# Issuing the r and v loads of the first three steps from the ScalarE DMA queue in a fused RWKV-6 and squared-ReLU kernel

## The chip, the cores and the metric

The kernel runs on one core of one Trainium2 chip. The metric is the device time in microseconds of that core. A profile of one execution gives the span from the first to the last instruction, which is a little shorter than the device time.

## The reference

Two layers are computed one after the other. The first is a linear attention with a decaying state (B, H, S, D = 4, 8, 768, 48):

```python
for t in range(S):
    cur = einsum('bhd,bhe->bhde', u[None] * kt, vt)
    y[:, :, t] = einsum('bhd,bhde->bhe', rt, state + cur)
    state = wt[:, :, :, None] * state + einsum('bhd,bhe->bhde', kt, vt)
```

Its output is laid out as 3072 tokens by 384 and goes through `maximum(x @ w_in, 0)`, a square, and `@ w_out`, with w_in 384 x 2048 and w_out 2048 x 384. All inputs and outputs are float32.

## The kernel before, in words

The attention is worked off in 24 steps, each one chunk of 128 tokens of one batch entry with all eight heads: six steps follow one another through the state, then the next batch entry begins. A step needs four loads of 192 KB, w, r, k and v, in rows of 48 floats (192 bytes). Its work is cut into small functions, one per engine and stage:

- ScalarE: `lw_` (L149, logarithm of w), `exp_` (L184 and L185), `v_` (L153, v to bf16), `xt_` (L273, the finished chunk into `xT`).
- PE: `cum_` (L176 to L179, cumulative sums of the logarithm), `tr_` (L198), `p_` (L210), `su_` (L225), `y_` (L247, L255), `yt_` (L270).
- DVE: `rd_` (L189), `rkt_` (L202), `pm_` (L216), `ts_` (L232, L234), `q_` (L165), `ysb_` (L261).
- GpSimd (POOL): `ku_` (L157), `qp_` (L161), `vq_` (L169), `sn_` (L238).

The second layer works on blocks of one or two finished chunks: `m1_` (L288, PE) gives groups of 512 columns of hidden values, `rl_` (L295, ScalarE) takes the ReLU, `gt_` (L300, DVE) the square, `m2_` (L307, PE) the second product in four quarters, `os_` (L312, ScalarE) the copy out of PSUM, and `store` (L316) writes 192 KB. A first-layer matmul over a block of two chunks has 256 columns ("wide"), over one chunk 128 ("narrow"). `m1_` has two PSUM buffers, so its third group needs the ReLU of the first.

The weights come in eight loads of 768 KB, four of w_in (`load_wi`, L95) and four of w_out (`load_wo`, L101), and are cast to bf16 by `cast` (L108); the first and third of each go to ScalarE, the second and fourth to DVE.

All loads and stores are issued on SyncE (SP), in one row. The loads stand in the order of `seq`: w, r, k, v of step 0, u, the four of step 1, four of w_in, the four of step 2, four of w_out, then step after step. `A_IN = 7` buffers hold each raw input.

The order of all engines' work is made while the program is built. `op` enters each piece with its engine, an assumed duration, a rank and what it depends on; `make_order` then plays the engines forward in time, gives each free engine its lowest-ranked ready piece, and writes down the resulting order, which each engine later follows instruction by instruction. A load on SP is assumed to take 1.25 us (2.08 for weights) and to be there when it ends. Where PE would stand idle before the first `m2_`, `warm_` matmuls (L321), whose result is not used, are put in.

Of the kernel before, what the change touches and what calls it, by code (L numbers as in the profile page):

```python
# [9 lines left out]
FP32 = mybir.dt.float32  # L10
# [7 lines left out]
def kernel(  # L18
# [11 lines left out]
    nc = tc.nc  # L30
    PSUM = bass.MemoryType.PSUM

    B, H, S, D = r.shape
    C = 128
# [10 lines left out]
    A_IN = 7  # L45
    HOP = .2
    PACE = 0.0

    nc.scalar.preload_act_table_set("natural_log_exp_and_others")

# [3 lines left out]
    a_in = ctx.enter_context(tc.tile_pool(name="a_in", bufs=A_IN))  # L54
# [10 lines left out]
    ps_m2 = ctx.enter_context(tc.tile_pool(name="ps_m2", bufs=1, space=PSUM))  # L65


    def load_one(dst, src, b, c):
        nc.sync.dma_start(  # L69
            out=dst, in_=src[b, :, c * C:(c + 1) * C, :].rearrange("h c d -> c h d"))  # L70

    raw = {}

    def load_step(step, part):
        b, c = divmod(step, NCH)
        if part == "w":
            raw["w", step] = a_in.tile([C, H, D], FP32, name="w_raw")
            load_one(raw["w", step][:], w, b, c)
        elif part == "r":
            raw["rk", step] = a_in.tile([C, 2, H, D], FP32, name="rk_raw")  # L80
            load_one(raw["rk", step][:, 0], r, b, c)
        elif part == "k":
            load_one(raw["rk", step][:, 1], k, b, c)
        else:
            raw["v", step] = a_in.tile([C, H, D], FP32, name="v_raw")
            load_one(raw["v", step][:], v, b, c)

    wi_sb = weights.tile([C, KT, DFF], BF16)
    wo_sb = weights.tile([C, NT, DM], BF16)
# [238 lines left out]
    def op(eng, us, rank, fn, args, deps, take=None, give=None):  # L328
        key = (fn.__name__,) + args
        plan[key] = (eng, us, rank, fn, args, deps, take, give)  # L330

    def steps(s, *names):
        return [(n, s) for n in names] if s >= 0 else []

    for s in range(NSTEP):
        c, at = s % NCH, s * 100
# [25 lines left out]
    for kind, cols in (("i", KT), ("o", 4)):  # L362
        for g in range(4):
            for j in range(cols):
                eng = "AV"[g % 2]
# [29 lines left out]
    def ld(n, x):  # L395
        {"i": load_wi, "o": load_wo}.get(x, lambda g: load_u() if x == "u" else load_step(g, x))(n)

    last = []
    for n, x in seq:
        free = steps(n - A_IN, *{"w": ("lw_",), "r": ("rd_", "qp_"), "v": ("v_", "vq_")}.get(x, ()))  # L400
        op("S", {"i": 2.08, "o": 2.08, "u": .65}.get(x, 1.25), 0, ld, (n, x), last + free)
        last = [("ld", n, x)]

    def make_order():
        hop, pace, pace_from = HOP, PACE, 5
        free_at = dict(P=0.0, V=0.0, A=1.5, G=0.0, S=2.35)
        psum = {x: [0.0] * n for x, n in dict(cp=1, tr=1, y=1, m1=2, m2=1, rl=3).items()}
        waits = {k: [d for d in plan[k][5] if d in plan] for k in plan}
        todo = {e: sorted((k for k in plan if plan[k][0] == e), key=lambda k: plan[k][2])
                for e in free_at}  # L410
        done, order, times, next_cum = {}, [], [0.0, 1.5, 2.35], 0.0
        while any(todo.values()):
            now = heapq.heappop(times)
            for e in free_at:
                if free_at[e] > now + 1e-6:
                    continue
                for key in todo[e]:
                    _, us, _, fn, _, _, take, give = plan[key]
                    deps = waits[key]
                    if any(d not in done or  # L420
                           done[d] + (hop if plan[d][0] != e else 0) > now + 1e-6 for d in deps):
                        continue
                    if take and not (psum[take] and min(psum[take]) < now + 1e-6):
                        continue
                    if fn is cum_ and key[1] >= pace_from:
                        if now < next_cum - 1e-6:
                            heapq.heappush(times, next_cum)
                            continue
                    if fn is cum_:
                        next_cum = now + pace  # L430
                    if take:
                        psum[take].remove(min(psum[take]))
                    end = done[key] = free_at[e] = now + us
                    if give:
                        psum[give].append(end + hop)
                        heapq.heappush(times, end + hop)
                    heapq.heappush(times, end)
                    heapq.heappush(times, end + hop)
                    order.append((now, key))
                    todo[e].remove(key)  # L440
                    break
        first_m2 = min(t for t, k in order if k[0] == "m2_")
        at = 0.0
        for t, key in [x for x in order if plan[x[1]][0] == "P"]:
            if at < first_m2:
                n = int((t - at - .1) / (.215 if at > 7 else .43))
                if n > 0 and t <= first_m2:
                    order.append((at + 1e-4, ("warm_", n)))
            at = done[key]
        return sorted(order, key=lambda x: x[0]), done  # L450

    order, done = make_order()
    E = mybir.EngineType
    with tc.manual_schedule(engines={E.PE, E.DVE, E.Activation, E.Pool, E.SP}):
# [34 lines left out]
```

## Time and profile before

| | us |
|---|---|
| device time, median of 2 runs | 219.09 (218.32 to 219.87) |
| span of the profiled execution | 214.2 |
| PE busy, share of the span | 197.1 (92%) |
| PE busy with `warm_` matmuls (L321) | 17.9 |
| DVE busy | 152.7 (71%) |
| ACT busy | 127.5 (60%) |
| POOL busy | 84.1 (39%) |
| chain that ended last: PE, SP's queue, DMA, DVE | 46%, 13%, 13%, 10% |
| first `m1_` matmul begins | 21.65 |
| last step load is issued | 142.11 |

The profiled execution's own device time is not listed apart from the two runs; the median stands 4.9 us above the span. "Busy" counts the time in which an engine works on an instruction. An instruction that issues a DMA is not counted as busy; it is shown under SPq for SyncE. L numbers are lines of the kernel before. A share of the DMA engines is the mean over 16 of them, and can pass 1 in a short stretch, since the packets of a transfer overlap.

### The profile page before, as it was taken

The page shows a single profiled execution, that of the slowest core. Times are in us where ns is not written, and L with a number is a line of the kernel's source. Part 1 is how long each engine was busy: PE and PEld are TensorE (multiplying, and loading weights), DVE is VectorE, ACT ScalarE, POOL GpSimd, SP SyncE. Part 2 cuts the span into 40 slices and gives each one's busy share as a digit, 9 for nine tenths or more (in the row PEclk, how much of TensorE's full clock was granted, in tenths as well). Part 3 has the DMA queues.
Part 4 walks back from the last instruction along what each step waited for, and adds up shares of the span by engine and source line. Part 5 has one row for each costly group of instructions (what it writes and reads, how often), then busy time and mean ns, then how long its engine had stood idle before and what let it go on. Part 6 is the DMA issues. An engine that isn't in the chain of part 4 may idle for free.

```text
span 214.2 us, 5655 instructions
## 1 busy us (share of the span) xinstructions
PE 197.1 (92%) x2232; PEld 140.4 (66%) x2232; DVE 152.7 (71%) x279; ACT 127.5 (60%) x255; POOL 84.1 (39%) x105
## 2 busy tenths in 40 slices
PE   7898997987899997989999999999999999999983
PEld 2454765555677675766766677777777777777751
DVE  3475795646898989879859989989886775533310
ACT  3353966644856767477685576667847546555540
POOL 5371320546556639655565655557112010000000
PEclk9999999999999999999999999999999999999999
DMA  7999899779987999699889997983101100111112
GB/s 135 195 307 344 207 383 219 153 164 193 177 152 150 181 163 171 135 200 160 172 167 195 142 203 147 193 176 76 40 2 41 37 11 28 40 37 37 40 37 73
DMA packets 107177, 30.43 MB, mean 142 GB/s; under 512 B 100368, under 2 KB 105616, under 8 KB 107152
## 3 DMA queue, kind: packets, MB, share of 16 engines
q1 hardware_dynamic: 107152, 30.09, 67.1%
q8 instruction: 17, 0.28, 0.6%
q14 instruction: 8, 0.07, 0.1%
HBM read 25.36 MB, written 4.72 MB: 140 GB/s over the span
## 4 chain that ended last, share of the span: by engine, by line
PE 46%; SPq 13%; DMA 13%; DVE 10%; issue 7%; POOL 6%; ACT 3%; DVEq 0%; POOLq 0%
PE m L307 19%; PE m L288 17%; SPq L69 10%; DMA w_st<-in_moe_w_out_dram 4%; DVE gt L300 4%; DMA w_raw<-in_w_dram 3%; DMA v_raw<-in_v_dram 3%; POOL qprod L161 2%; DVE pmT L216 2%; PE tr L198 2%; POOL ku L157 2%; DMA rk_raw<-in_r_dram 2%; POOL vq L169 2%; PE cp L210 1%; SPq L95 1%
## 5 line engine op out<-in xcount | busy, mean ns | idle before, releaser
L288 PE MATMUL m<-xT,wi_sb 128*128 128x256 bf16 (+1 forms) x672 | 76.5, 257 | 4.2 <-ACT xT L273 2.9
L295 ACT ACTIVATE rl<-m 128x512 f16<-128x512 f32 x96 | 56.5, 597 | 37.5 <-PE m L288 36.4
L307 PE MATMUL m<-wo_sb,gt 128*128 128x384 bf16 x384 | 74.9, 326 | 1.2 <-ACT o_sb L312 0.6
L288 PEld LDWEIGHTS <-wi_sb 128*128 128x128 bf16 x672 | 57.7, 98 | 17.1 <-issue 5.4
L300 DVE TENSOR_TENSOR gt<-rl 128x512 bf16<-128x512 f16 x96 | 54.7, 584 | 19.8 <-ACT rl L295 19.2
L307 PEld LDWEIGHTS <-gt 128*128 128x128 bf16 x384 | 35.3, 98 | 19.7 <-DVE gt L300 1.3
L157 POOL TENSOR_TENSOR ku<-rk_raw,u_bc 128x384 f32<-128x384 f32 x24 | 24.8, 1034 | 42.1 <-DMA rk_raw<-in_k_dram 37.3
L216 DVE TENSOR_TENSOR pmT<-cp,tri_strict 128x512 bf16<-128x512 f32 x48 | 30.8, 681 | 3.6 <-PE cp L210 3.6
L189 DVE TENSOR_TENSOR rdec_buf<-rk_raw,cp 128x768 bf16<-128x768 f32 x24 | 22.8, 948 | 11.2 <-ACT cp L185 9.0
L169 POOL TENSOR_TENSOR vq<-v_raw,q 128x384 f32<-128x384 f32 x24 | 21.6, 901 | 18.8 <-DVE y_sb L261 8.6
L161 POOL TENSOR_TENSOR qprod<-rk_raw,ku 128x384 f32<-128x384 f32 x24 | 25.1, 1048 | 1.2
L238 POOL TENSOR_TENSOR S<-t_state,a_c 128x192 bf16<-128x192 f32 x20 | 11.0, 548 | 29.3 <-DVE t_state L234 16.7
L185 ACT ACTIVATE cp<-cp 128x768 f32<-128x768 f32 x24 | 19.1, 795 | 0.8
L321 PE MATMUL m<-warm 128*128 128x512 bf16 x64 | 17.9, 416 | 1.2 <-DVE warm L129 1.2
L202 DVE COPY rkT<-tr 128x1024 bf16<-128x1024 bf16 x24 | 16.4, 682 | 3.7 <-PE tr L198 3.7
L149 ACT ACTIVATE lw_buf<-w_raw 128x384 bf16<-128x384 f32 x24 | 12.5, 521 | 8.4 <-DMA w_raw<-in_w_dram 8.2
L153 ACT CAST v_bf<-v_raw 128x384 bf16<-128x384 f32 x24 | 12.2, 508 | 8.4 <-DMA v_raw<-in_v_dram 7.7
L312 ACT ACTIVATE o_sb<-m 128x384 f32<-128x384 f32 x24 | 11.8, 491 | 8.2 <-PE m L307 7.6
L165 DVE TENSOR_REDUCE q<-qprod 128x8 f32<-128x384 f32 x24 | 13.1, 545 | 4.4 <-POOL qprod L161 4.1
L198 PE MATMUL tr<-ident,rdec_buf 128*128 128x128 bf16 x192 | 14.8, 220 | 1.3 <-DVE rdec_buf L189 1.0
L261 DVE TENSOR_TENSOR y_sb<-vq,y 128x384 bf16<-128x384 f32 x24 | 13.1, 547 | 2.2 <-PE y L255 2.1
L198 PEld LDWEIGHTS <-rdec_buf 128*128 128x128 bf16 x192 | 11.5, 98 | 4.1 <-DVE rdec_buf L189 2.0
(40 smaller groups left out, 142.9 us busy)
## 6 DMA issues: line engine op xcount, KB each, us to landing
w_raw<-in_w_dram SPq DMA_DIRECT2D x24, 192.0 KB, 4.3
rk_raw<-in_r_dram SPq DMA_DIRECT2D x24, 192.0 KB, 4.2
rk_raw<-in_k_dram SPq DMA_DIRECT2D x24, 192.0 KB, 4.3
v_raw<-in_v_dram SPq DMA_DIRECT2D x24, 192.0 KB, 4.1
out_dram<-o_sb SPq DMA_DIRECT2D x24, 192.0 KB, 2.0
w_st<-in_moe_w_in_dram SPq DMA_DIRECT2D x4, 768.0 KB, 8.5
w_st<-in_moe_w_out_dram SPq DMA_DIRECT2D x4, 768.0 KB, 8.6
u_bc<-in_u_dram SPq DMA_DIRECT2D x1, 192.0 KB, 4.6
```

The lines of the kernel that those rows point to most:

```text
L69: nc.sync.dma_start(out=dst, in_=src[b, :, c * C:(c + 1) * C, :].rearrange("h c d -> c h d"))
L157: nc.gpsimd.tensor_mul(ku[:], raw["rk", s][:, 1], u_bc[:])
L161: nc.gpsimd.tensor_mul(qp[:], raw["rk", s][:, 0], tiles.pop(("ku", s))[:])
L169: nc.gpsimd.tensor_mul(vq[:], raw["v", s][:], tiles.pop(("q", s))[:, :, None].to_broadcast([C, H, D]))
L185: nc.scalar.activation(cs[:, :, 0:DM], cs[:, :, 0:DM], AF.Exp)
L189: nc.vector.tensor_mul(rdec[:, :, :, 0:D], raw["rk", s][:], tiles.pop(("cs", s))[:, :, 0:DM].rearrange("p a (h d) -> p a h d", h=H))
L198: nc.tensor.transpose(ps_tr[:, i, p, :], rdec[:, i, 2 * p:2 * p + 2, :], ident[:])
L216: nc.vector.tensor_mul(tiles["pmT", s][:, e], tiles["p", s][:, e].rearrange("p (a t) -> p a t", a=HP), tri_strict[:, None, :].to_broadcast ...
L288: nc.tensor.matmul(ps1[:, j, :], wi_sb[:, kk, n * 128:(n + 1) * 128], xT[:, kk, s0 * C:s0 * C + width], start=(kk == 0), stop=(kk == KT - 1))
L295: nc.scalar.activation(rl[:], tiles.pop(("m1", i, g))[:], AF.Relu, scale=RS)
L300: nc.vector.tensor_mul(tiles["gt", i][:, g * ng:(g + 1) * ng, :], rl[:], rl[:])
L307: nc.tensor.matmul(tiles["m2"][:], gt[:, n, mt * 128:(mt + 1) * 128], wo_sb[:, n, :], start=(n == 0), stop=(n == NT - 1))
```

## The change

A constant `TWO = 3` names the first three steps. Their r and v loads are issued from ScalarE's DMA queue, and are planned there; w and k, and all later loads, stay on SP. In the plan such a load takes 0.5 us of ScalarE and is there 2.5 us later; v is entered as depending on r of its step.

```diff
+    TWO = 3
...
-    def load_one(dst, src, b, c):
-        nc.sync.dma_start(
+    def load_one(dst, src, b, c, eng=None):
+        (eng or nc.sync).dma_start(
...
         elif part == "r":
-            raw["rk", step] = a_in.tile([C, 2, H, D], FP32, name="rk_raw")
-            load_one(raw["rk", step][:, 0], r, b, c)
+            if ("rk", step) not in raw:
+                raw["rk", step] = a_in.tile([C, 2, H, D], FP32, name="rk_raw")
+            load_one(raw["rk", step][:, 0], r, b, c, nc.scalar if step < TWO else None)
         elif part == "k":
+            if ("rk", step) not in raw:
+                raw["rk", step] = a_in.tile([C, 2, H, D], FP32, name="rk_raw")
             load_one(raw["rk", step][:, 1], k, b, c)
         else:
             raw["v", step] = a_in.tile([C, H, D], FP32, name="v_raw")
-            load_one(raw["v", step][:], v, b, c)
+            load_one(raw["v", step][:], v, b, c, nc.scalar if step < TWO else None)
...
+        if x in "rv" and n < TWO:
+            op("A", .5, -100, ld, (n, x), [("ld", n, "r")] if x == "v" else [])
+            continue
         op("S", {"i": 2.08, "o": 2.08, "u": .65}.get(x, 1.25), 0, ld, (n, x), last + free)
...
-                    end = done[key] = free_at[e] = now + us
+                    end = free_at[e] = now + us
+                    if fn is ld and e == "A":
+                        end += 2.5
+                    done[key] = end
```

## The prediction

> **What bounds the kernel now.** I read the page first, then the waits and the chain, then the order of time of SP's queue and of ScalarE in the first 50 us, then the windows. The slices of the page (5.36 us each) give the outline:
>
> ```profile
> PE   7898997987899997989999999999999999999983
> ...
> DVE  3475795646898989879859989989886775533310
> ...
> DMA  7999899779987999699889997983101100111112
> ```
>
> There are three stages. Up to about 40 us the DMA engines are full and PE's digits contain stand-in work: L321's `warm` matmuls fill 17.9 us. From 60 to 117 us DVE is at 8 to 9. From 117 us PE is full and the chain holds only matmuls. So the end is set by how much useful matmul work PE has behind it when it becomes full. What is lost early is lost for good, unless PE later gets to work where it waits now.
>
> The windows of the start (columns: stretch, length, the granted clock, DMA busy share, GB/s) ask whether one issuing queue starves the DMA engines:
>
> ```profile
> 1.00:2.00 1.00, 1.00 0.07 15
> 2.00:3.00 1.00, 1.00 1.10 208
> 3.00:4.00 1.00, 1.00 1.13 215
> ...
> 15.00:16.00 1.00, 1.00 1.02 373
> ...
> 22.00:23.00 1.00, 1.00 0.48 96
> ```
>
> It does not: from 2.0 us the share is 1.0, small loads run at about 205 GB/s (192 KB in 0.96 us), weight loads at 370 to 400. Up to 35 us only the second at 22 us is half empty. The first nine loads have landed by about 11.9 us, (11.9 - 2.0) / 9 = 1.1 us each; a weight load takes about 2.4.
>
> ScalarE and SP in order of time show what the first useful block waits for:
>
> ```profile
> 12.30 5.18 SPq L69 DMA_DIRECT2D rk_raw<-in_r_dram  x1
> 17.53 4.29 SPq L69 DMA_DIRECT2D rk_raw<-in_k_dram  x1
> ...
> 20.09 1.14 ACT L108 CAST wi_sb<-w_st 128x512 bf16<-128x512 f32 x2 [3.18 <-DMA w_st<-in_moe_w_in_dram]
> ...
> 21.13 0.47 ACT L273 COPY xT<-tr 128x384 bf16<-128x384 bf16 x1
> ...
> 21.65 1.47 PE L288 MATMUL m<-xT,wi_sb 128*128 128x256 bf16 x12 [1.02 <-ACT xT L273]
> ```
>
> The second xT copy stands behind two casts that waited for the third w_in load; half a microsecond later `m1_` begins. SP's 5.18 and 4.29 us are r and k of step 2, held up while the weight loads drain. Then the chain between 38 and 49 us:
>
> ```profile
> 38.21 0.44 ACT o_sb L312
> 39.13 3.32 DMA w_raw<-in_w_dram
> 42.47 0.52 ACT lw_buf L149
> 42.99 0.39 ACT o_sb L312
> 43.80 2.99 DMA v_raw<-in_v_dram
> 46.81 0.51 ACT v_bf L153
> ```
>
> Here loads of step 4 stand behind a store on SP, and the store waits for its o_sb. That leaves holes in the DMA stream (share 0.29 in 38 to 40 us, 0.27 in 43 to 44).
>
> **What the Trainium skill says.** "DMA: Bandwidth & Descriptors", section "Issuing engines are not separate DMA queues": loads from different engines run on the same 16 DMA engines, and several issuers save only "the time on the sequencer it takes to initiate the DMA". The trace agrees as far as it goes: with one issuer the share is already 1.0 from 2 us. The same page, "Queues, rings and completion order": each DMA engine alternates between the queues packet by packet. No run here shows it yet; I use it for the landing order. The section "Anatomy of one DMA — SWDGE (gpsimd) path" says that a semaphore wait is spent on the issuing sequencer. So a load that waits blocks its engine; the chain above shows that on SP.
>
> **The change part by part.** Time does not follow from the diff alone: the planner now counts six loads off SP, so it reorders every engine. I read the built instruction order.
>
> *Issues.* Six loads leave SP and six join ScalarE. On SP they cost 0.57, 0.85, 0.61, 0.70, 5.18 and 0.61 us, but with the DMA engines full nothing starts earlier: gain at the front 0, at most the 0.5 us hole at 22 us. On ScalarE I take 0.6 to 0.85 us each, 4.3 in all. Low end: hidden, since ScalarE is busy 5.6 of the first 15 us. High end: r2's 5.18 if an issue gets stuck here too.
>
> *Waits on ScalarE.* The build gives all loads eight completion semaphores in turn, and a load waits for the previous user of its own. ScalarE's queue begins: table load, r0, r1, r2, v0 (waits for w0), `lw_`(0), v1 (waits for u), `exp_`(0), v2 (waits for w1), `lw_`(1), `v_`(0), `v_`(1), `exp_`(1). The table load ends at 2.01, three issues end at 4.3, v0 at 5.0, so `lw_`(0) starts at 5.0 for 3.83. u is third on SP beside r0 and r1 and lands near 8 (8.1 before), so `exp_`(0) goes from 5.94 to 8.8. w1 lands near 10; v1 near 14.5, since r2 and v0 share the engines with it; `exp_`(1) starts near 15 for 12.1. By itself this is hidden, because of the next item.
>
> *First `m1_`.* On PE `cum_`(2) now stands ahead of `yt_`(1) and the first `m1_`; on ScalarE all six w_in casts, then `lw_`(2), xT(0), `exp_`(2), stand ahead of xT(1). So w of step 2 now gates it, and w2 lands after all w_in. Before, w2 landed at 11.75 + 10.9 = 22.65. Now r2 and v2 move ahead of it: 2 x 1.1 = 2.2, so 24.9. Then lw 0.52, `cum_` 0.6, a_c and exp 1.0, xT 0.47, with 0.1 to 0.2 between engines: 28.0 for 21.65, **6.3 us later**.
>
> *To 46 us.* ScalarE next places four casts of the first w_out load, three relus, and four casts of the third w_out load (landing 33.35 before, and the same bytes lie ahead of it now). With two `m1` buffers PE gets five groups out and waits until about 35.9. `cum_`(3) follows at 36.8, then `m2_`. Following both orders with the trace's durations, at 46 us both are at `su_`(4). Before has done 48 wide and 48 narrow `m1` matmuls and 44 `m2`; after has 48, 36 and 16. The gap is 12 x 0.056 + 28 x 0.163 = **5.2 us of PE work**.
>
> *Recovery to `cum_`(6).* In both orders the same MLP work stands ahead of it: 90 wide-equivalent `m1` and 48 `m2`. After, left from 46.1 us: 24 x 0.11 + 32 x 0.163 = 7.9 of MLP and about 3.5 of attention, so 57.5 without a wait. Before was there at 55.86, with up to 3 us of waits on the way. The loads of steps 4 and 5 now come before the first store (22 step loads ahead of it, not 16), so I charge 1.1 us of waits: 58.6, **+2.7**. Ends: 1.6 and 5.
>
> *`cum_`(6) to `cum_`(12).* Before this took 39.6 us, with DVE work of 6 x 4.37 + 19 x 0.584 = 37.3 (the page's means: rdec 0.948, rkT 0.682, two pmT 1.362, q 0.545, y_sb 0.547, and t_state 0.35 in five steps of six). After has 18 squares: 36.7, so -0.6. But 1.9 us less MLP stands ahead of `cum_`(12) (198 and 100, not 204 and 108), and stays for the PE-bound rest: **+1.3**.
>
> *Stores further back.* Every store now has 2 to 9 more loads ahead of it, which shortens stalls like those in the chain. DVE waits 3.3 us for qprod between 60 and 120 us, and qprod waits for k's load; I credit a quarter, **-0.8**. Ends: 0 and the 6.6 us that DVE is idle there.
>
> Sum: 2.7 + 1.3 - 0.8 = +3.2. The profiled span of 214.2 becomes 217.4. The median of 219.09 has 4.9 us more than that span around it; kept, this is **222.3 us**.
>
> **Rivals.** *Nothing lasting (219.5).* The late start is absorbed: PE waits about 7 us between 46 and 120 us (8.2 from 40 us on, by the windows, some 1 of it before 46). For it: the 5.2 us deficit is mostly `m2`, needing neither ScalarE nor DVE at its start. Against it: queues are fixed, and DVE is near full in that stretch.
>
> *Faster (about 217.2).* Mechanism: stores no longer hold up loads. Place: SP, 38 to 110 us. Price: PE's 7.1 us of waits there, all gone: 5.2 - 7.1 = -1.9. It decides from the point where more than the 5.2 us comes back. For it: the chain above, and the stores' new places. Against it: much of that waiting is for DVE's own work.
>
> *Much slower (227).* An issue on ScalarE gets stuck as on SP (5.18 us) and holds `lw_`(1), `exp_`(1) and the casts, or late loads meet orders planned for early ones all through: 3 to 6 us more. For it: the weights' queue is deep at 10 us. Against it: until w2 lands near 25 there is slack of several microseconds.
>
> The change not doing what it says is excluded by the built order: the six loads are on ScalarE.
>
> **How the numbers follow.** Main case (2 to 6 us lost, 221 to 225, centre 222.3): 0.50. Much slower: 0.20. Nothing lasting: 0.18. Faster: 0.12. 2% is 4.4 us, about what a measurement of this kernel can tell from no change: limits 214.7 and 223.5. Slower: all of 0.20 and two fifths of 0.50, 0.40. Faster: a third of 0.12, 0.04. Rest 0.56. The range leaves out most of the faster case and the upper half of the much slower one: 217.0 to 228.0.
>
> **What would show it.** Right: DMA share still 1.0 from 2 us, the six issues on ScalarE, `exp_`(0) near 8.8, w2 near 25, the first `m1_` near 28 and directly after xT(1), third w_out landing unmoved near 33, PE behind by about 5 us of `m2` at 46. From 60 us DVE as full as before. Wrong: first `m1_` at 22 to 24, or PE without waits between 46 and 100 us, or loads landing more than 1 us earlier up to 35 us.

## The result, and the profile after

The changed kernel took 225.01 us (median of 2 runs, 223.59 to 226.43) against 219.09 before. The ratio is 1.0379, with a 95% interval of 1.0269 to 1.0489; it is made from undisturbed executions alone, so it is not the quotient of these medians. A later repetition gave 1.035 (1.0302 to 1.0399). The profiled span grew from 214.2 to 221.6 us, by 7.4, where 3.2 had been forecast. The profiled execution of the changed kernel took 223.59, so 2.0 us lie around its span, and not the 4.9 that the prediction had added from the median of before.

The slices of the page after (5.54 us each). L numbers of profiles after are lines of the changed kernel; from `cast` on they are four higher than in the kernel before.

```profile
PE   7560999996998888999999999997999999999983
...
DVE  3322689975878987999988998697775875333310
...
PEclk9966799999999999999999999999999999999999
DMA  8999999718979989969968969960111010100101
GB/s 133 209 356 306 330 328 171 126 38 144 190 148 166 199 144 196 176 145 176 188 139 182 201 141 189 198 130 0 38 37 38 1 38 36 38 36 36 38 36 71
```

Three things are new. PE's fourth slice (17 to 22 us) is empty, and the granted clock falls to 0.6 and 0.7 around it. DMA falls to a share of 0.1 in the ninth slice (44 to 50 us), where the kernel before has 0.85. And PE is not full for good from 117 us, but only from about 155: between 149 and 155 us it is busy 4.57 of 6 us, where the kernel before has 6.00.

The windows of the start (stretch, length, granted clock, DMA share, GB/s) answer those of before:

```profile
1.00:2.00 1.00, 1.00 0.07 14
2.00:3.00 1.00, 1.00 0.99 183
3.00:4.00 1.00, 1.00 1.29 247
15.00:16.00 1.00, 1.00 1.09 350
22.00:23.00 1.00, 0.50 1.46 200
```

A second issuing queue brings no more data per microsecond at the start; only the hole at 22 us is filled. This is what the Trainium skill's "DMA: Bandwidth & Descriptors", section "Issuing engines are not separate DMA queues", leads one to expect. What changes is which bytes come first. The order of time on ScalarE (ACTq are the issues, the brackets give the idle time before an instruction and what ended it):

```profile
7.64 0.38 ACTq L70 DMA_DIRECT2D v_raw<-in_v_dram  x1
...
9.25 0.76 ACTq L70 DMA_DIRECT2D v_raw<-in_v_dram  x1
...
19.29 0.51 ACT L157 CAST v_bf<-v_raw 128x384 bf16<-128x384 f32 x1 [7.07 <-DMA v_raw<-in_v_dram]
...
19.91 0.80 ACT L189 ACTIVATE cp<-cp 128x768 f32<-128x768 f32 x1
...
22.78 0.51 ACT L157 CAST v_bf<-v_raw 128x384 bf16<-128x384 f32 x1 [2.08 <-DMA v_raw<-in_v_dram]
...
23.20 3.21 ACT L112 CAST wi_sb<-w_st 128x512 bf16<-128x512 f32 x6
```

v of step 1 is issued at 7.64 and needs 11.6 us to land, v of step 2 13.5; before, v of step 1 took 4.0. The cast of the first stands ahead of the exp of step 1, which is otherwise ready, and the cast of the second stands ahead of all six w_in casts. The first `m1_` begins at 31.16 us instead of 21.65, 9.5 us later. Then SP's queue:

```profile
40.36 0.77 SPq L70 DMA_DIRECT2D rk_raw<-in_r_dram  x1
47.97 0.36 SPq L320 DMA_DIRECT2D out_dram<-o_sb  x1
48.37 1.70 SPq L70 DMA_DIRECT2D rk_raw<-in_k_dram  x1
```

SP reaches the first store at 41.1 us and waits there for its o_sb until 47.97; k of step 5 and all that follows stand behind it. The chain of waits after shows what comes of it:

```profile
47.45 0.50 ACT o_sb L316
47.95 0.02 issue
47.97 0.36 SPq L320
48.33 0.04 issue
48.37 1.70 SPq L70
50.07 0.04 issue
50.12 3.62 DMA v_raw<-in_v_dram
53.74 0.02 issue
53.76 0.51 ACT v_bf L157
54.27 0.38 ACT xT L277
54.65 0.41 ACT o_sb L316
55.06 0.02 issue
55.07 0.36 SPq L320
```

It is a loop: o_sb, store, load, cast, o_sb, store. It is there in the kernel before too, but here it runs about nine microseconds later.

### The profile page after: what moved, and what is told of

The parts are those of the page before. It is cut to its first block, busy times and chain, and to the rows that moved or that the text cites. A ratio compares the mean times of both kernels' runs of the same rounds, so it can differ in the third digit from the quotient of the medians.

```text
span 221.6 us, 5628 instructions
## 1 busy us (share of the span) xinstructions
PE 199.0 (90%) x2226; PEld 141.4 (64%) x2230; DVE 151.6 (68%) x279; ACT 126.3 (57%) x255; POOL 83.1 (38%) x105
## 4 chain that ended last, share of the span: by engine, by line
PE 42%; DMA 17%; issue 14%; POOL 13%; DVE 9%; SPq 2%; ACT 2%; POOLq 0%; DVEq 0%
PE m L292 15%; PE m L311 14%; DMA v_raw<-in_v_dram 9%; POOL qprod L165 5%; POOL ku L161 4%; PE m L325 4%; DMA rk_raw<-in_k_dram 4%; POOL vq L173 3%; DVE gt L304 3%; DMA u_bc<-in_u_dram 3%; PE tr L202 2%; DVE rdec_buf L193 2%; SPq L70 2%; DMA rk_raw<-in_r_dram 2%; DVE pmT L220 2%
## 5 line engine op out<-in xcount | busy, mean ns | idle before, releaser
L299 ACT ACTIVATE rl<-m 128x512 f16<-128x512 f32 x96 | 56.4, 597 | 45.2 <-PE m L292 41.1
L304 DVE TENSOR_TENSOR gt<-rl 128x512 bf16<-128x512 f16 x96 | 51.2, 550 | 21.0 <-ACT rl L299 20.8
L311 PEld LDWEIGHTS <-gt 128*128 128x128 bf16 x384 | 35.6, 98 | 18.3 <-issue 1.1
L161 POOL TENSOR_TENSOR ku<-rk_raw,u_bc 128x384 f32<-128x384 f32 x24 | 24.9, 1037 | 34.4 <-DMA rk_raw<-in_k_dram 30.1
L193 DVE TENSOR_TENSOR rdec_buf<-rk_raw,cp 128x768 bf16<-128x768 f32 x24 | 22.7, 947 | 17.6 <-ACT cp L189 16.4
L173 POOL TENSOR_TENSOR vq<-v_raw,q 128x384 f32<-128x384 f32 x24 | 20.5, 856 | 30.4 <-DVE q L169 13.6
L165 POOL TENSOR_TENSOR qprod<-rk_raw,ku 128x384 f32<-128x384 f32 x24 | 24.9, 1036 | 1.6
L325 PE MATMUL m<-warm 128*128 128x512 bf16 x58 | 18.9, 452 | 1.6 <-DVE warm L133 1.2
L206 DVE COPY rkT<-tr 128x1024 bf16<-128x1024 bf16 x24 | 16.4, 681 | 2.7 <-PE tr L202 2.7
L214 PE MATMUL cp<-rkT 64*128 64x128 bf16 x192 | 9.7, 221 | 7.9 <-DVE rdec_buf L193 7.4
L202 PEld LDWEIGHTS <-rdec_buf 128*128 128x128 bf16 x192 | 11.6, 100 | 6.2 <-DVE rdec_buf L193 4.1
```

The costliest lines, as they stand in the source:

```text
L161: nc.gpsimd.tensor_mul(ku[:], raw["rk", s][:, 1], u_bc[:])
L165: nc.gpsimd.tensor_mul(qp[:], raw["rk", s][:, 0], tiles.pop(("ku", s))[:])
L173: nc.gpsimd.tensor_mul(vq[:], raw["v", s][:], tiles.pop(("q", s))[:, :, None].to_broadcast([C, H, D]))
L193: nc.vector.tensor_mul(rdec[:, :, :, 0:D], raw["rk", s][:], tiles.pop(("cs", s))[:, :, 0:DM].rearrange("p a (h d) -> p a h d", h=H))
L202: nc.tensor.transpose(ps_tr[:, i, p, :], rdec[:, i, 2 * p:2 * p + 2, :], ident[:])
L299: nc.scalar.activation(rl[:], tiles.pop(("m1", i, g))[:], AF.Relu, scale=RS)
```

## The experiments

Twelve runs followed. Two theories stood against each other first. The queue: the moved loads land late and ScalarE waits for them. The plan: every engine's order is now made for loads that are there 7.5 us sooner than they can be (six loads of 1.25 us counted off SP). Ratios are to the kernel before on the same chip.

**The queue without the plan, first try.** The old planned order; only the issuing engine is changed.

```diff
-        nc.sync.dma_start(
+        (eng or nc.sync).dma_start(
...
+            load_one(raw["rk", step][:, 0], r, b, c, nc.scalar if step < 3 else None)
...
+            load_one(raw["v", step][:], v, b, c, nc.scalar if step < 3 else None)
```

> The old planned order of all compute, with the six loads issued from ScalarE at their old places in that order. Queue theory (the loads' packets take turns with the weight loads, and ScalarE waits): v of step 1 lands near 20 us as in the changed kernel, and the time is near 225. Plan theory (what costs is the new order, made for loads that are there 7.5 us earlier): 219, within 1 us. My own reading lies between: v of step 1 late, but no exp stands behind its cast in the old order, so the first m1 begins at 23 to 25 and the time is 220.5 to 222.5.

Measured: 225.49 to 232.63 in four runs, too scattered for a ratio. In its profile v of step 0 is issued behind the exp of step 0 at 6.62 and lands at 18.3, r and v of step 1 are issued only behind its cast, and the first `m1_` begins at 38.2. My reading was far too low: in the old order the issues themselves stood in bad places. So this run doesn't part queue and plan, and I repeated it with the issues where the changed kernel has them.

**The queue without the plan, second try.** The same, with r0, r1, r2 and v0 ahead of the first `lw_`, v1 ahead of the first `exp_`, v2 ahead of the second `lw_`.

> The old planned order of all compute, with the six issues on ScalarE at the places that they have in the changed kernel (the queue without the plan). If late v loads act through what stands behind their casts, v of step 1 lands at 19.3 as in the changed kernel, the w_in casts begin at 19.8 instead of 14.5, the first m1 at 23.5 to 25, and the loss is 0.5 to 1.5 per cent. Theory that the queue alone makes the loss: 3 per cent or more. Theory that the plan alone makes it: none.

Measured: v of step 1 lands at 19.35 again, the w_in casts begin at 19.77, the first `m1_` only at 26.61, and the ratio is 1.019 (1.0131 to 1.0249). Neither the theory of the queue alone nor that of the plan alone holds. The loss is a little above my range, though its interval reaches into it; `m1_` began 1.6 us after its own.

**The plan without the queue.** The changed kernel's order of all compute, with the loads on SP in their old sequence.

```diff
...
+    first = [("ld", n, x) for n, x in seq[:17]]
+    order = [(0, key) for key in first] + [x for x in order if x[1] not in first]
```

> The new planned order of all compute, with all loads on SP in their old sequence. Queue theory: v of step 1 lands near 12 as before, PE has no hole from 13 to 21 us, and the time is near 219 to 220. Plan theory: near 225. My reading: exp of step 1 at 12 to 13, but the casts of w_in stand behind the cast of v of step 2, which lands at about 25, so the first m1 begins near 30 and the time is 223 to 225.

Measured: 228.04 us, ratio 1.0574 (1.053 to 1.0618), worse than the changed kernel. ScalarE shows my mechanism and its place:

```profile
12.46 0.80 ACT L189 ACTIVATE cp<-cp 128x768 f32<-128x768 f32 x1
25.16 0.51 ACT L157 CAST v_bf<-v_raw 128x384 bf16<-128x384 f32 x1 [11.90 <-DMA v_raw<-in_v_dram]
```

The exp is on time, and then everything waits 11.9 us for the v of step 2, which comes behind w_in on SP. The first `m1_` begins at 32.87. So the new order costs by itself, and more when the loads are where they used to be: given this order, the ScalarE queue helps. The two losses do not add up: the queue alone makes 1.9%, the plan alone 5.7%, both together 3.5%. I had put it at 223 to 225, too low.

**The two casts moved back.**

```diff
...
+    for x, y in ((("v_", 1), ("exp_", 1)), (("v_", 2), ("xt_", 1))):
+        order.remove(x)
+        order.insert(order.index(y) + 1, x)
...
```

> The changed kernel with two casts moved back on ScalarE: v of step 1 behind exp of step 1, v of step 2 behind the second xT copy. If it is these two late loads ahead of ready work that cost, exp of step 1 starts near 11.5 instead of 19.9, PE's hole from 13 to 21 us goes, the first m1 begins near 27.5 to 28.5 instead of 31.2, and 2 to 3 us come back: 222 to 223. Plan theory: unchanged within 1 us, 224 to 226. Issue theory (ScalarE's time for issuing costs): unchanged too.

Measured: exp of step 1 at 12.26, first `m1_` at 25.75 (better than expected), ratio 1.0259 (1.0181 to 1.0337). By the ratios some 2 us of the changed kernel's loss come back, the low end of what was expected, and the interval still touches that of the changed kernel. v of step 1 still lands at 19.2: for the start, what costs is not only that it is late but what stands behind it.

**v on SP ahead of w_in, r on ScalarE, the new plan kept.**

```diff
...
+    vs = [("ld", n, "v") for n in range(TWO)]
+    order = [key for _, key in order if key not in vs]
+    at = order.index(("ld", 0, "i"))
+    order[at:at] = vs
...
```

> The changed kernel's plan, r of the three steps on ScalarE, but the three v loads on SP ahead of w_in. If taking turns with the weight loads is what makes v late, v of step 1 and 2 land within 5 us of their issue (by 11 to 14 us) instead of 11.6 and 13.5, exp of step 1 starts near 12.5, the first m1 begins at 24 to 26 (held by w of step 2, whose landing stays near 24), and the loss falls to 1 to 2.5 per cent. Plan theory (orders made for early loads cost all through): still 3 per cent or more, whatever the first m1 does.

Measured: the three v land 4.5 to 7.1 us after their issue, that of step 1 by 12.9; exp of step 1 at 13.47; first `m1_` at 26.41; ratio 1.017 (1.010 to 1.0241). Issued ahead of the weight loads, v of step 1 is 6.4 us earlier, and half of the loss is gone. What is left of the delay waits for w of step 2 (lw at 23.75), the gate that the prediction had named.

**The changed kernel once more.**

> The changed kernel unaltered, to stand beside the others on the same chip. All theories: 3 to 4.5 per cent above the kernel before, and the first m1 at 31, as in its first profile.

Measured: 224.72 us, ratio 1.035 (1.0302 to 1.0399), first `m1_` at 31.86.

**Without the warm matmuls behind the second `cum_`** (left out; their result is not used).

> The changed kernel without the warm matmuls behind the second cumulative sum (their result is not used). They were planned into planned idle time and stand ahead of ready work in the changed kernel, at a reduced granted clock; its chain holds 3.8 per cent of them. If they delay the start, the first m1 begins 1.5 to 3 us earlier and as much is gained. If they keep the clock up for what follows, the granted clock is lower between 15 and 35 us and the time is the same or up to 3 us longer. Theory that only the late v counts: within 1 us.

Measured: 222.75 us, ratio 1.0244 (1.0178 to 1.031), about 2 us better than the changed kernel. The first `m1_` begins 2.3 us earlier, as the first half of the expectation says. The granted clock is lower, as the second half says, but the time is not longer for it.

```profile
29.60 2.72 PE L292 MATMUL m<-xT,wi_sb 128*128 128x256 bf16 x12 [1.17 <-ACT xT L277]
```

The same twelve take 1.47 us in the changed kernel. The delay weighed more than the clock.

**How the queues share: rows of w_in of 512 bytes, and the control.** Both cut each w_in load in three parts; one writes rows of 512 bytes, the other 2048.

> The changed kernel with each w_in load cut in three and written in rows of 512 bytes instead of 2048. If the queues take turns packet by packet, v of step 1 (192-byte packets) gets 27 per cent of the bytes instead of 9, and lands 4 to 6 us after its issue instead of 11.6. If the queues share by bytes or by time, it lands 9 to 12 us after its issue as before.

> Control of the run with 512-byte rows: w_in in the same three parts and the same waits, rows of 2048 bytes. If the size of the packets decided there, v of step 1 takes 11 to 13 us from issue to landing here, against 6.9. If the cut into three parts decided, 6 to 8 us here too.

Measured: v of step 1 lands 6.9 us after its issue with 512 bytes, 8.6 with 2048, 11.6 uncut. Both values with parts lie between the ranges of the two theories, so neither is borne out. Most of the difference from the uncut case is the later issue (9.5 and 9.3 instead of 7.6). A fairer measure is the time from the landing of v of step 0 to that of step 1: 4.5 us, 6.0 and 7.6, that is 43, 33 and 26 GB/s for 192 KB. One row for one row would give 192/2240, 9% of the 346 GB/s at that time, 30 GB/s: near the uncut case. The packets of the changed kernel's trace say the same: from 12 to 19 us SP's queue moved 1164 and ScalarE's 1096, nearly one for one. For 512 bytes it would give 27% of some 270, 73 GB/s, and 43 were measured; there SP's queue moved 2037 packets beside 1040 (12 to 16.4 us). The Trainium skill says in "DMA: Bandwidth & Descriptors", "Queues, rings and completion order", that an engine drains a whole packet of one queue, of several descriptors, before it switches; the direction agrees, the rule for the shares stays open. These are single runs, without a ratio: 224.57 and 222.69 us, with the first `m1_` at 28.27 and 28.18.

**One step only** (`TWO = 1`).

> TWO = 1: only r and v of step 0 go to ScalarE, planned anew. Both land before the weight loads begin, and the plan is only 2.5 us too early. My reading: v of step 0 not later than 8, the first m1 near 22 to 23.5, and 218 to 221. Plan theory by proportion: a third of the loss, 221. Queue theory: 219 to 220, as nothing competes with the weights.

Measured: 216.57 us against 216.21, ratio 1.0031 (1.0005 to 1.0056). v of step 0 is cast at 10.06, later than I had said; the first `m1_` begins at 20.73, 0.9 us earlier than before. Earlier at the start does not make the end earlier: at `cum_`(6) this kernel is already 1.8 us behind the one before.

**The stores on ScalarE**, behind their o_sb, once in the kernel before and once in the changed one.

```diff
-        nc.sync.dma_start(out=out[t0:t0 + C, :], in_=tiles.pop(("o", i, mt))[:])
+        nc.scalar.dma_start(out=out[t0:t0 + C, :], in_=tiles.pop(("o", i, mt))[:])
```

> The kernel before with the 24 stores issued from ScalarE behind their o_sb copy, so that no load stands behind a store on SP. If stores that hold up loads cost in the middle (as the chain between 38 and 49 us says), 1 to 4 us come back: 213 to 216 against 217. If DVE's own work bounds the middle anyway, within 1 us. If 24 issues of 0.4 us weigh on ScalarE, up to 2 us slower.

> The changed kernel with the same stores on ScalarE. In it SP waits from 41 to 48 us at the first store, while DMA runs at a share of 0.3. If this matters, it gains at least as much as the kernel before does from the same edit, 2 to 5 us. If the late start alone sets its end, the same gain as there or less.

Measured: 214.63 us, ratio 0.9885 (0.9799 to 0.9972), and 216.40 us, ratio 0.9997 (0.9974 to 1.002). In the changed kernel the edit is worth 3.5% (1.035 to 0.9997), some 7.6 us, more than the 2 to 5 expected; in the kernel before it is worth 1.15%, under the 2% limit but with an interval below 1. The start is as late as ever (first `m1_` at 31.68). The stretches 41 to 47 and 48 to 60 us, first of the changed kernel, then of the same with its stores on ScalarE (columns as above; the kernel before has a share of 0.88 in the first):

```profile
41.00:47.00 6.00, 1.00 0.36 68
48.00:60.00 12.00, 1.00 0.77 154
```

```profile
41.00:47.00 6.00, 1.00 0.97 185
48.00:60.00 12.00, 1.00 1.03 206
```

The waits between 40 and 155 us, again first of the changed kernel and then with its stores on ScalarE (engine and line, releaser, us in total, times, longest):

```profile
POOL ku L161 <- DMA rk_raw<-in_k_dram: 28.7, 15, 4.1
ACT rl L299 <- PE m L292: 18.6, 19, 2.3
POOL vq L173 <- DVE q L169: 11.9, 9, 3.8
ACT v_bf L157 <- DMA v_raw<-in_v_dram: 8.6, 6, 3.0
```

```profile
ACT rl L299 <- PE m L292: 23.1, 25, 2.4
POOL vq L173 <- DVE y_sb L265: 17.2, 8, 4.6
POOL vq L173 <- DVE q L169: 15.4, 8, 3.8
```

The waits of ku and v_bf for loads are no longer among the long ones. They are no mark of the changed kernel alone, though: in the kernel before, ku waits 25.1 us for its loads and v_bf 7.7. With loads free to run ahead, the 24th step's `cum_` starts at 168.8 us, in the changed kernel at 175.9 (in its repetition at 176.8). This compares ends only between kernels of one plan: the kernel before starts its 24th step at 176.4 and ends 7.4 us before the changed one, since less of its second layer is left.

What decides is how much of this PE feels. PE's busy time (after the stretch each line has its length, the busy time and the number of matmuls, then the clock, the DMA share and GB/s) from 46 to 155 us, in the order before, changed, before with stores moved, changed with stores moved:

```profile
46.00:155.00 109.00, 101.54 (x1285) 1.00 0.89 161
46.00:155.00 109.00, 101.30 (x1277) 1.00 0.87 157
46.00:155.00 109.00, 104.91 (x1324) 1.00 0.86 159
46.00:155.00 109.00, 107.48 (x1362) 1.00 0.81 155
```

PE idles 7.5 us in this stretch before and 7.7 in the changed kernel, so the change adds hardly any waiting there. Up to 46 us it adds 5.2 (10.9 for 5.7). With the stores moved the idle time of the stretch falls to 4.1 and 1.5. So the stores do not make new waits in the changed kernel; they keep waits in which PE could catch up on its late start.

Start and end together, in the order of the first `m1_`:

| kernel | first `m1_` | `cum_`(6) | ratio |
|---|---|---|---|
| TWO = 1 | 20.73 | 57.7 | 1.0031 |
| before | 21.65 | 55.9 | 1 |
| casts moved back | 25.75 | 57.7 | 1.0259 |
| v on SP | 26.41 | 57.8 | 1.017 |
| old plan, new queue | 26.61 | 61.2 | 1.019 |
| fewer warm matmuls | 29.60 | 60.4 | 1.0244 |
| changed, repeated | 31.86 | 62.2 | 1.035 |
| new plan, old queue | 32.87 | 64.2 | 1.0574 |
| before, stores moved | 20.97 | 56.8 | 0.9885 |
| changed, stores moved | 31.68 | 60.6 | 0.9997 |

The two columns of times come from one profiled execution of each kernel; for the casts moved back and for v on SP this was the fastest one. With stores on SP a later start goes with a later end, but only roughly: the kernels that start between 25.8 and 29.6 us lie between 1.7 and 2.6% in no order, and their intervals overlap. With stores on ScalarE a start 10.7 us later costs 1.1% (some 0.2 to 2.0, an estimate from the two intervals).

## Why the prediction was right or wrong

The prediction had the direction right, and a late start as its cause. On the span it had less than half of the loss.

*What bounds the kernel*, and no gain from a second queue at the front: right. Share and bytes are as before. Some large loads did land over 1 us earlier (the third of w_in at 18.8 for 20.1, the third of w_out at 31.7 for 33.3), which had been named as a sign of being wrong; small loads landed later instead, so the bytes had only changed places. Of DVE the prediction read its own line loosely: it has a slice of 5 near 110 us, and 8 or 9 go on to about 155.

*Issues*: right. They took 2.46 us for three, then 0.99, 0.38 and 0.76, 4.6 in all for 4.3 forecast. None got stuck, so the first mechanism of the much slower rival did not come.

*Waits on ScalarE*: `lw_`(0) at 5.48 for 5.0 and `exp_`(0) at 8.26 for 8.8, right. v of step 1 was mis-sized: landing 19.3, not 14.5. I had let it share with r2 and v0 and forgotten the weight loads, which SP issues from 6.49. "By itself this is hidden" fell with it. PE had a hole in place of work.

*First `m1_`*: 9.5 us later, not 6.3, and held by something else. w of step 2 landed at 23.1, before the 24.9 forecast, and its `lw_` did not wait for it. ScalarE was behind: it stood at v of step 2 until 22.78, with the six casts after that; warm matmuls delayed PE at a reduced clock. Putting v out of the way took 5.5 us off the repetition's first `m1_`, moving two casts 6.1, leaving out warm matmuls 2.3. These overlap.

*To 46 us*: the right quantity, too small. At 46.1 us the changed kernel had done 48 wide, 28 narrow and 12 `m2` matmuls, where 48, 36 and 16 stood; the kernel before 48, 48 and 46. With the prediction's prices the gap is 20 x 0.056 + 34 x 0.163 = 6.7 us, not 5.2.

*Recovery to `cum_`(6)*: 61.70, not 58.6, so +5.8 instead of +2.7. This is the largest miss of the sum. The work that was left had been put too low: 56 x 0.056 + 36 x 0.163 = 9.0 us of MLP for 7.9, and some 4.8 of attention for 3.5 (what remains of the 15.5 us from 46.1 when the MLP and 1.7 of idle time are taken off). PE idled 1.7 us for 1.1 charged. 22 loads do stand ahead of the first store, but the store came at 47.97 instead of 38.73, and SP, through with the 22 at 41.1, moved nothing for 7 us. This standstill is not what makes the miss: with the stores moved `cum_`(6) begins only 1.1 us sooner, at 60.6. Its price comes later.

*`cum_`(6) to `cum_`(12), and stores further back*: 61.70 to 99.09, 37.4 us for 39.6 before, and 1.9 us less MLP done. That leaves the lag at 3.6 + 1.9 = 5.5: on balance -0.3 where +1.3 - 0.8 = +0.5 stood. The credit for the stores was wrong in sign all the same. Moving them shortens this stretch by 3.1 us in the changed kernel (37.4 to 34.3) and by 0.6 in the one before (39.6 to 39.0), so they hold the changed kernel back more, not less. Later places help only while the plan keeps time; here compute was 9 us behind.

*After `cum_`(12)* the prediction had put nothing, and the last 1.9 us of the 7.4 arose there. PE idles 6.7 us from there to the end for 5.5 before. Of this 1.4 fall between 149 and 155 us (0.6 in the repetition), where it waits for `y_sb` and `rdec_buf` of DVE; the kernel before has no wait there. The other 0.7 us stay open.

Over the whole run moving the stores is worth 3.5% in the changed kernel and 1.15% in the one before. So of the loss of some 3.5%, about 1.1% is what the late start costs with the stores out of the way; the rest needs the stores on SP.

*Rivals.* Nothing lasting was ruled out as the kernels stand, and is nearly right with the stores moved. The faster rival named the right place, SP from 38 to 110 us, and took it for a gain: it was there to be had, but not by this change. The much slower rival had named a second mechanism, late loads meeting orders that were planned for early ones. It came, at the start, with v of steps 1 and 2; PE does not wait more than before all through.

*How the numbers follow*: 222.3 was +3.2 us on the span, 1.5%; +7.4 was measured, 3.5%. Adding 4.9 for what lies around the span, instead of the 2.0 measured, carried the sum 2.9 us towards the 225.01 that was measured; that it came this near is in part luck. The direction and the idea, a late start that is only partly made up, held. The sizes of the start, of the work left at 46 us and of the stores did not.

What stays open: how the two queues share the DMA engines when the large rows are shorter, why the plan with the old queue ends 2% to 3% behind kernels that start only 1 to 3 us sooner, and whether the stores cost by their wait on SP alone or also by sharing its queue. The best version found is the kernel before with its stores on ScalarE, 1.15% faster than the kernel before.

## What to carry to other kernels

When a planned order is made for earlier data, ask first whether the data can come earlier at all: here, with the DMA engines full, a second queue only changed which bytes came first, and the small loads beside large ones came late. Then look at what stands behind each late load on its engine. And a store that stands ahead of loads in one queue ties the loads to the pace of the compute: in these kernels a delay that could have been made up then lasted to the end.

## What the runs showed of the hardware that was not expected

A load of 192 KB in rows of 192 bytes, issued on ScalarE's queue while SP's queue moved w_in, got 26 GB/s of 346 and took 11.6 us, while the two queues moved packets nearly one for one (1164 of SP's, nearly all of 2048 bytes, beside 1096 of ScalarE's, 12 to 19 us); issued on SP ahead of w_in such loads took 4.5 to 7.1. Towards the end of PE's hole the granted clock fell: it was 0.50 from 20 to 25 us in the changed kernel and in its repetition. Without warm matmuls it was 0.50 from 15 to 30 us, where twelve real matmuls took 2.72 us instead of 1.47.
